# A decode step with cached attention: the first head's K in two pairs of tiles, and the scores' maximum as a running elementwise maximum

## The chip, the core and the metric

The kernel runs on one core of one Trainium2 chip. The metric is the device time of one execution in microseconds (us). A core has several engines that run beside each other: TensorE (PE) multiplies matrices, VectorE (DVE) does elementwise work, reductions and 32x32 transposes, ScalarE (ACT) does casts and functions such as the exponential, and SyncE (SP) issues the large transfers from the chip's memory into the on-chip buffer (SBUF). The transfers themselves are moved by 16 DMA engines. Matrix products land in PSUM, a small accumulation memory.

## What is computed

One token goes through two branches and a gate. Branch A is attention with 32 query heads that share 4 K/V heads of 65536 cached positions each, branch B is a gated MLP. The cut reference:

```python
def _A_ref(x, k_cache, v_cache, wq, wo):          # x 1x1x1024, caches 1x4x65536x128
    q = (x @ wq).reshape(B, Sq, 32, 128).transpose(0, 2, 1, 3)
    k = jnp.repeat(k_cache, 8, axis=1)
    v = jnp.repeat(v_cache, 8, axis=1)
    scores = jnp.einsum('bhqd,bhkd->bhqk', q, k) * 128 ** (-0.5)
    p = softmax(scores, axis=-1)
    o = jnp.einsum('bhqk,bhkd->bhqd', p, v)
    return o.transpose(0, 2, 1, 3).reshape(B, Sq, 4096) @ wo     # wo 4096x1024
...
g = sigmoid((x * gate_w).sum(-1, keepdims=True))
a = _A_ref(x, A_k_cache, A_v_cache, A_wq, A_wo)
b = _B_ref(x, B_w_in, B_w_sp, B_b_sp, B_w_out)    # gelu, layernorm, two products
return g * a + (1 - g) * b
```

All inputs are bf16. K and V together are 134 MB, the weights 28 MB.

## The kernel before

All large inputs pass through one SBUF buffer `kv` with five slots of one tile each. A tile is 128 partitions x 16384 bf16 elements, 4.19 MB; a K head is four tiles (`j` = 0 to 3), and so is a V head. `load(src, shape, at)` starts a transfer into the buffer at slot `at`; `load_kv(src, g, j, at, n)` loads `n` adjacent tiles of head `g`, beginning with tile `j`, in one transfer. Every load is issued by SP in program order, and a load waits until what the slots held before has been used.

```python
P = 128; CT = 128; NKV = 5
kv = big.tile([P, NKV * CT * P], BF16, name="kv")

def load(src, shape, at):
    ...
    ins = nc.sync.dma_start(out=v, in_=src)          # L184

def load_kv(src, g, j, at, n=1):
    h, i = divmod(j, 2)
    rows = src[0, g, 2 * h * CT * P:2 * (h + 1) * CT * P, :].rearrange(
        "(p c) d -> p (c d)", c=2 * CT)
    v = load(rows[:, i * CT * DH:(i + n) * CT * DH], (n * CT * DH,), at)
    return [v[:, i * CT * DH:(i + 1) * CT * DH] for i in range(n)]
```

The first loads are the weights: `B_w_in` at slot 3 (it fills slots 3 and most of 4) and `A_wq` at slots 0 and 1. TensorE uses each as soon as it has landed (`z_ps`, then `q_ps`).

A K tile is worked on in four quarters (`VC` = 4): DVE transposes a quarter in place in blocks of 32x32, reading pairs of bf16 as one int32, and TensorE multiplies it with the query weights `wt`. ACT casts the scores of the tile from PSUM to a bf16 tile `sc` of 128x1024. The row maximum of that tile is taken by DVE with `reduce_max`, put off (`late`) until after the next tile's first transpose.

```python
def k_tile(g, j, kn):
    s_ps = pss.tile([P, 2 * HN], FP32, name="s_ps", tag="s")
    for v in range(VC):
        nc.vector.transpose(out=kb[:, v * n:(v + 1) * n], in_=kb[:, v * n:(v + 1) * n])   # L403
        while late:
            nc.vector.reduce_max(**late.pop())                                            # L405
        for b in range(BP):
            for k in range(2):
                ins = nc.tensor.matmul(s_ps[:, k * HN:(k + 1) * HN], lhsT=wt[...], rhs=kx[...])  # L410
    if g not in mxs:
        mxs[g] = wk.tile([P, NT], FP32, name="mx")
    sct[g, j] = scp.tile([P, CC * B], BF16, name="sc")
    nc.scalar.copy(out=sct[g, j][:], in_=s_ps[:])                                         # L421
    late.append(dict(out=mxs[g][:, j:j + 1], in_=sct[g, j][:], axis=AX.X))
```

When a head's four tiles of scores are there, `stats(g)` brings the maximum of each query row into `nb`, takes the exponential of the four tiles on ACT, and transposes them on DVE for the product with V:

```python
def stats(g):
    nc.vector.reduce_max(**late.pop())                              # L425
    m1 = wk.tile([P, 1], FP32, name="m1")
    nc.vector.reduce_max(out=m1[:], in_=mxs[g][:], axis=AX.X)       # L427
    # PE transpose, max over partitions (L431), copy (L434), PE broadcast, scale (L439) -> nb
    for j in range(NT):
        nc.scalar.activation(out=sct[g, j][:], in_=sct[g, j][:], func=ACT.Exp, ...)   # L443
        nc.vector.transpose(out=ptt[g, j], in_=sct[g, j][:])        # L446
```

`v_tile` (L456, TensorE alone) multiplies these with a V tile, and `head_out` finishes a head. The order of the program:

```python
build_w(0)
for j, n, at in ((0, 1, 2), (1, 1, 3), (2, 1, 0), (3, 1, 1)):
    for i, kn in enumerate(load_kv(A_k_cache, 0, j, at, n)):
        k_tile(0, j + i, kn)
    if j == 1:
        build_w(1)
project(load(B_w_out..., (FC, D), 4), FC, uT, 0, first=True)
stats(0)
for g in range(1, G):
    for h in range(2):
        kn = load_kv(A_k_cache, g, 2 * h, 2 + h, 2)        # slots 2,3 and then 3,4
        for i in ((1, 0), (0, 1))[h]:
            k_tile(g, 2 * h + i, kn[i])
        if h == 0 and g + 1 < G:
            build_w(g + 1)
        vn = load_kv(A_v_cache, g - 1, 2 * h, 0, 2)        # slots 0,1
        v_tile(g - 1, 2 * h, vn[0])
        if h == 1:
            stats(g)
        v_tile(g - 1, 2 * h + 1, vn[1])
    head_out(g - 1)
# ... the last head's V, then A_wo in five pieces
```

Of the kernel before, what the change touches and what calls it, by code (L numbers as in the profile page):

```python
# [8 lines left out]
FP32 = mybir.dt.float32  # L9
BF16 = mybir.dt.bfloat16  # L10
I32 = mybir.dt.int32
ACT = mybir.ActivationFunctionType
ALU = mybir.AluOpType
AX = mybir.AxisListType

P = 128
CT = 128
NKV = 5
B = 32
NB = P // B  # L20
VC = 4
CC = CT // VC
# [7 lines left out]
def kernel(  # L30
# [15 lines left out]
    nc = tc.nc  # L46
# [12 lines left out]
    NT = S // (P * CT)  # L59
# [9 lines left out]
    wk = ctx.enter_context(tc.tile_pool(name="wk", bufs=2))  # L69
    big = ctx.enter_context(tc.tile_pool(name="big", bufs=1))  # L70
# [9 lines left out]
    def same_weights(ins):  # L80
        held.add(ins.ins.name)
# [95 lines left out]
    def load(src, shape, at):  # L177
        n = 1
        for s in shape:
            n *= s  # L180
        v = kv[:, int(at * CT * P):int(at * CT * P) + n]
        if len(shape) == 2:
            v = v.rearrange("p (a b) -> p a b", b=shape[1])
        ins = nc.sync.dma_start(out=v, in_=src)  # L184
        if not first_load:
            first_load.append(ins.ins.name)
        return v
# [7 lines that stand above are left out]
# [60 lines left out]
    for t in range(2):  # L255
        nc.vector.tensor_tensor(  # L256
            out=xm[:, t], in0=xb_ps[:, t * P:(t + 1) * P].rearrange("p (i c) -> p c i", c=KC),
            in1=sel_i[:].unsqueeze(1).to_broadcast([P, KC, P // KC]), op=ALU.mult)
# [51 lines left out]
    for hf in range(2):  # L310
        nc.vector.tensor_tensor(
            out=zm[:, hf], in0=z_ps[:, hf * HN:hf * HN + ZN].rearrange("p (j c) -> p j c", c=FC),
            in1=own_b[:].unsqueeze(2).to_broadcast([P, B, FC]), op=ALU.mult)
    z = wk.tile([P, 2 * FC], FP32, name="z")
    nc.vector.tensor_reduce(out=z[:].rearrange("p (h c) -> p h c", h=2),
                            in_=zm.rearrange("p h j c -> p h c j"), axis=AX.X, op=ALU.add)
# [24 lines left out]
                            op=ALU.subtract)  # L341
# [19 lines left out]
    for k in range(NHB):  # L361
        xs = slice(k * NX // NHB, (k + 1) * NX // NHB)
        nc.vector.tensor_tensor(  # L363
            out=qm[:, xs], in0=q_ps[:, k * HN:(k + 1) * HN].rearrange("p (x j e) -> p x j e",
                                                                   j=B, e=2),
            in1=own_b[:].unsqueeze(1).unsqueeze(3).to_broadcast([P, NX // NHB, B, 2]), op=ALU.mult)
    q1 = wk.tile([P, NX, 2], FP32, name="q1")
    nc.vector.tensor_reduce(out=q1[:], in_=qm.rearrange("p x j e -> p x e j"), axis=AX.X,
                            op=ALU.add)
    q4 = wk.tile([P, NB, NX * 2], BF16, name="q4")  # L370
    nc.vector.tensor_tensor(
        out=q4[:], in0=q1[:].rearrange("p x e -> p (x e)").unsqueeze(1).to_broadcast(
            [P, NB, NX * 2]),
        in1=own_n[:].unsqueeze(2).to_broadcast([P, NB, NX * 2]), op=ALU.mult)
# [6 lines left out]
    for g in range(G):  # L381
        k, t0 = g * T2 // NB, g * T2 % NB
        nc.vector.tensor_copy(out=qs[:, g].rearrange("p b (t h) -> p b t h", t=T2),
                              in_=qv[:, k, t0:t0 + T2].rearrange("p t h b -> p b t h"))

    def build_w(g):
        for v in range(VC):
            nc.vector.tensor_tensor(
                out=wt[g % 2][:, v, :, :, v, :],
                in0=qs[:, g].unsqueeze(2).to_broadcast([P, BP, NB, REP]),  # L390
                in1=own_n[:].unsqueeze(1).unsqueeze(3).to_broadcast([P, BP, NB, REP]),
                op=ALU.mult)

    oa = const.tile([P, OC], BF16, name="oa")
    late = []
    sct, ptt, mxs, lss, o_ps = {}, {}, {}, {}, {}

    def k_tile(g, j, kn):
        kb = kn.bitcast(I32)
        n = CC * DH // 2  # L400
        s_ps = pss.tile([P, 2 * HN], FP32, name="s_ps", tag="s")
        for v in range(VC):
            nc.vector.transpose(out=kb[:, v * n:(v + 1) * n], in_=kb[:, v * n:(v + 1) * n])  # L403
            while late:
                nc.vector.reduce_max(**late.pop())  # L405
            kx = kn[:, v * CC * DH:(v + 1) * CC * DH].rearrange(
                "p (c h k e) -> p h e c k", h=2, k=B, e=2)
            for b in range(BP):
                for k in range(2):
                    ins = nc.tensor.matmul(  # L410
                        s_ps[:, k * HN:(k + 1) * HN],
                        lhsT=wt[g % 2][:, v, b].rearrange("p a v h -> p (a v h)"),
                        rhs=kx[:, b // 2, b % 2, k * CC // 2:(k + 1) * CC // 2, :],
                        start=(v == 0 and b == 0), stop=(v == VC - 1 and b == BP - 1),
                        skip_group_check=True)
                    if k > 0:
                        same_weights(ins)
        if g not in mxs:
            mxs[g] = wk.tile([P, NT], FP32, name="mx")
        sct[g, j] = scp.tile([P, CC * B], BF16, name="sc")  # L420
        nc.scalar.copy(out=sct[g, j][:], in_=s_ps[:])  # L421
        late.append(dict(out=mxs[g][:, j:j + 1], in_=sct[g, j][:], axis=AX.X))

    def stats(g):
        nc.vector.reduce_max(**late.pop())  # L425
        m1 = wk.tile([P, 1], FP32, name="m1")
        nc.vector.reduce_max(out=m1[:], in_=mxs[g][:], axis=AX.X)  # L427
        mt_ps = psm.tile([1, P], FP32, name="mt_ps", tag="m")
        nc.tensor.transpose(mt_ps[:], m1[:], ident_f[:])
        gm = wk.tile([1, REP], FP32, name="gm")  # L430
        nc.vector.tensor_reduce(out=gm[:], in_=mt_ps[:].rearrange("p (a h) -> p h a", h=REP),  # L431
                                axis=AX.X, op=ALU.max)
        gr = wk.tile([1, P // REP, REP], FP32, name="gr")
        nc.vector.tensor_copy(out=gr[:], in_=gm[:].unsqueeze(1).to_broadcast([1, P // REP, REP]))  # L434
        nb_ps = psm.tile([P, 1], FP32, name="nb_ps", tag="m")
        nc.tensor.matmul(nb_ps[:], lhsT=gr[:].rearrange("p a h -> p (a h)"),
                         rhs=ones_f[0:1, 0:1], start=True, stop=True)
        nb = wk.tile([P, 1], FP32, name="nb")
        nc.vector.tensor_scalar(out=nb[:], in0=nb_ps[:], scalar1=-SCALE, scalar2=None,  # L439
                                op0=ALU.mult)  # L440
        lss[g] = wk.tile([P, NT], FP32, name="ls")
        for j in range(NT):
            nc.scalar.activation(out=sct[g, j][:], in_=sct[g, j][:], func=ACT.Exp, scale=SCALE,  # L443
                                 bias=nb[:, 0:1], accum_out=lss[g][:, j:j + 1])
            ptt[g, j] = ptp.tile([P, CC, B], BF16, name="pt")
            nc.vector.transpose(out=ptt[g, j][:].rearrange("p c x -> p (c x)"),  # L446
                                in_=sct[g, j][:])
# [64 lines left out]


    build_w(0)
    for j, n, at in ((0, 1, 2), (1, 1, 3), (2, 1, 0), (3, 1, 1)):
        for i, kn in enumerate(load_kv(A_k_cache, 0, j, at, n)):
            k_tile(0, j + i, kn)
        if j == 1:
            build_w(1)
    project(load(B_w_out.rearrange("(p c) n -> p c n", c=FC), (FC, D), 4), FC, uT, 0, first=True)  # L520
    stats(0)
    for g in range(1, G):
        for h in range(2):
            kn = load_kv(A_k_cache, g, 2 * h, 2 + h, 2)
# [4 lines that stand above are left out]
            vn = load_kv(A_v_cache, g - 1, 2 * h, 0, 2)  # L529
# [5 lines that stand above are left out]
# [61 lines left out]
```

## Time and profile before

| what | value |
|---|---|
| device time, median of 3 (lowest to highest) | 382.2 us (382.17 to 382.49) |
| span of the profiled execution | 380.7 us |
| busy: PE, DVE, ACT | 233.2, 218.5, 39.6 us |
| moved by DMA | 162.17 MB, mean 426 GB/s |
| K and V loads issued by SP: of one tile, of two | 6, 13 |

Busy time is the time in which an engine executed instructions; engines overlap, so the shares do not add up. The rate of the DMA engines is the sum over the 16 of them. In the chain of waits the trace is followed backwards from the last instruction, each time to what released it; a piece "DMA kv" in it runs from the issue of a transfer to its landing, and so contains the time in which the transfer stood in the queue behind earlier ones. In the timeline, a line gives the start and duration of an instruction or of a run of equal ones, and in brackets how long the engine had been idle before it and on what it waited.

### The profile page before, as it was taken

To read this page: it belongs to the slowest core of one execution; us is meant where nothing else is said; L and a number is where in the kernel's file an instruction comes from. 1 tells how busy PE (TensorE), PEld (TensorE's weight loads), DVE (VectorE), ACT (ScalarE), POOL (GpSimd) and SP (SyncE) were. 2 spreads that over 40 slices of the span, in tenths; PEclk is the share of its full clock that TensorE was granted. 3 is DMA by queue.
4 is the path that set the end of the run, shared out by engine and by line. 5 is a ranking of instruction groups with operands and counts; after the bars stand their busy time and mean duration, and the time that the engine had idled before them with its cause. 6 is when DMAs were issued, how large, how long until landed. Compare 5 with 4: busy or idle time off the path is not lost.

```text
span 380.7 us, 2605 instructions
## 1 busy us (share of the span) xinstructions
PE 233.2 (61%) x1395; PEld 56.0 (15%) x800; DVE 218.5 (57%) x211; ACT 39.6 (10%) x55; POOL 4.4 (1%) x10
## 2 busy tenths in 40 slices
PE   0060657876157944796397729871977196839386
PEld 0010101111101210111011101120211011202113
DVE  4133288997597506966977059669970388460040
ACT  1001001110601100114010001050100000500000
POOL 4000000000000000000000000000000000000000
PEclk9995769899759895989688958895989579969789
DMA  9998999999999999999999999999999999999995
GB/s 386 496 420 379 411 438 441 437 483 430 387 420 441 441 436 441 427 441 441 434 436 441 441 427 434 406 423 441 434 434 429 420 441 442 436 410 430 424 443 223
DMA packets 3943, 162.17 MB, mean 426 GB/s; under 512 B 472, under 2 KB 476, under 8 KB 860
## 3 DMA queue, kind: packets, MB, share of 16 engines
q1 hardware_dynamic: 3892, 162.01, 98.8%
q8 instruction: 8, 0.13, 0.1%
q14 instruction: 3, 0.02, 0.0%
q10 hardware_dynamic: 40, 0.01, 0.0%
HBM read 162.01 MB, written 0.00 MB: 426 GB/s over the span
## 4 chain that ended last, share of the span: by engine, by line
DMA 57%; PE 26%; DVE 13%; ACT 2%; issue 1%; SPq 1%; DVEq 0%; ACTq 0%
DMA kv<-in_A_k_cache_dram 43%; PE s_ps L410 21%; DMA kv<-in_A_wo_dram 7%; DVE kv L403 7%; DMA kv<-in_A_v_cache_dram 7%; PE o_ps L456 4%; DVE pt L446 2%; DVE o_sb L470 1%; DVE mx L405 1%; ACT sc L421 1%; ACT sc L443 1%; DVE rowt L466 1%; SPq L184 1%; PE om_ps L476 0%; DVE osum L486 0%
## 5 line engine op out<-in xcount | busy, mean ns | idle before, releaser
L410 PE MATMUL s_ps<-kv,wt 128*128 128x512 bf16 x512 | 141.8, 437 | 80.2 <-DVE kv L403 80.2
L403 DVE STREAM_TRANSPOSE kv<-kv 128x2048 int32<-128x2048 int32 x64 | 142.7, 2281 | 54.3 <-DMA kv<-in_A_k_cache_dram 54.3
L456 PE MATMUL o_ps<-kv,pt 128*64 128x512 bf16 x512 | 61.7, 400 | 7.6 <-DMA kv<-in_A_v_cache_dram 7.6
L410 PEld LDWEIGHTS <-wt 128*128 128x128 bf16 x256 | 27.6, 108 | 195.6 <-issue 138.5
L421 ACT CAST sc<-s_ps 128x1024 bf16<-128x1024 f32 x16 | 16.2, 1012 | 249.9 <-PE s_ps L410 249.9
L456 PEld LDWEIGHTS <-pt 128*64 128x64 bf16 x256 | 16.1, 115 | 50.6 <-issue 48.1
L446 DVE STREAM_TRANSPOSE pt<-sc 128x1024 bf16<-128x1024 bf16 x16 | 18.6, 1217 | 6.8 <-ACT sc L443 6.8
L405 DVE TENSOR_REDUCE mx<-sc 128x1 f32<-128x1024 bf16 x12 | 14.5, 1210 | 9.9 <-ACT sc L421 9.9
L443 ACT ACTIVATE sc<-sc,nb 128x1024 bf16<-128x1024 bf16 x16 | 18.2, 1137 | 12.3 <-DVE nb L439 12.2
L466 DVE TENSOR_TENSOR rowt<-o_ps,own 128x1024 f32<-128x1024 f32 x4 | 4.8, 1195 | 24.9 <-PE o_ps L456 24.9
L476 PE MATMUL om_ps<-o_sb,hsel 128*32 128x128 f32 x8 | 2.3, 386 | 18.3 <-DVE o_sb L470 18.3
L425 DVE TENSOR_REDUCE mx<-sc 128x1 f32<-128x1024 bf16 x4 | 4.9, 1220 | 13.6 <-ACT sc L421 13.6
L296 PE MATMUL q_ps<-kv,xT 128*32 128x512 bf16 x64 | 5.6, 527 | 7.2 <-DMA kv<-in_A_wq_dram 7.2
L252 PE MATMUL xb_ps<-xg,spread 8*128 8x256 bf16 x1 | 0.4, 366 | 13.2 <-DMA xg<-in_gate_w_dram 13.2
L470 DVE TENSOR_REDUCE o_sb<-rowt 128x128 f32<-128x1024 f32 x4 | 7.5, 1872 | 0.1
L363 DVE TENSOR_TENSOR rowt<-q_ps,own_b 128x512 f32<-128x512 f32 x2 | 1.3, 686 | 10.8 <-PE q_ps L296 10.8
L296 PE MATMUL z_ps<-kv,xT 128*32 128x448 bf16 x64 | 5.9, 560 | 0.0
L495 PE MATMUL busy_ps<-wt 128*128 128x512 bf16 x23 | 5.8, 381 | 0.1
L506 PE MATMUL out_ps<-kv,oa 128*32 128x256 bf16 x128 | 4.2, 274 | 2.0 <-DMA kv<-in_A_wo_dram 2.0
L256 DVE TENSOR_TENSOR xm<-xb_ps,sel_i 128x128 f32<-128x128 f32 x2 | 0.5, 287 | 8.0 <-PE xb_ps L252 8.0
L552 ACT CAST out_sb<-out_ps 128x256 bf16<-128x256 f32 x1 | 0.4, 372 | 45.1 <-PE out_ps L506 45.1
L296 PEld LDWEIGHTS <-xT 128*32 128x32 bf16 x64 | 2.6, 136 | 14.6 <-issue 14.6
(90 smaller groups left out, 59.3 us busy)
## 6 DMA issues: line engine op xcount, KB each, us to landing
kv<-in_A_k_cache_dram SPq DMA_DIRECT2D x4, 4096.0 KB, 35.4
kv<-in_A_v_cache_dram SPq DMA_DIRECT2D x2, 4096.0 KB, 26.0
kv<-in_B_w_in_dram SPq DMA_DIRECT2D x1, 7168.0 KB, 19.4
kv<-in_A_wo_dram SPq DMA_DIRECT2D x1, 6144.0 KB
kv<-in_B_w_out_dram SPq DMA_DIRECT2D x1, 3584.0 KB
kv<-in_A_wo_dram SPq DMA_DIRECT2D x1, 1024.0 KB
kv<-in_A_wo_dram SPq DMA_DIRECT2D x1, 512.0 KB
kv<-in_A_wo_dram SPq DMA_DIRECT2D x2, 256.0 KB, 28.2
```

Source lines behind the costliest of these rows:

```text
L296: ins = nc.tensor.matmul(ps[t * B:(t + 1) * B, k * HN:k * HN + n], lhsT=xT[:, i * KH + c:i * KH + c + 1].to_broadcast([P, B]), rhs=w[:, c, ...
L403: nc.vector.transpose(out=kb[:, v * n:(v + 1) * n], in_=kb[:, v * n:(v + 1) * n])
L405: nc.vector.reduce_max(**late.pop())
L410: ins = nc.tensor.matmul(s_ps[:, k * HN:(k + 1) * HN], lhsT=wt[g % 2][:, v, b].rearrange("p a v h -> p (a v h)"), rhs=kx[:, b // 2, b % 2, ...
L421: nc.scalar.copy(out=sct[g, j][:], in_=s_ps[:])
L425: nc.vector.reduce_max(**late.pop())
L443: nc.scalar.activation(out=sct[g, j][:], in_=sct[g, j][:], func=ACT.Exp, scale=SCALE, bias=nb[:, 0:1], accum_out=lss[g][:, j:j + 1])
L446: nc.vector.transpose(out=ptt[g, j][:].rearrange("p c x -> p (c x)"), in_=sct[g, j][:])
L456: ins = nc.tensor.matmul(o_ps[g][hs, e, :], lhsT=ptt[g, j][:, 2 * u:2 * u + 2, :].rearrange("p c x -> p (c x)"), rhs=vx[:, 2 * u + e], sta ...
L466: nc.vector.tensor_tensor(out=om8, in0=o_ps[g][:].rearrange("p e (v d) -> p (e v) d", d=DH), in1=own_8[:].unsqueeze(2).to_broadcast([P, 2 ...
L470: nc.vector.tensor_reduce(out=o_sb[:], in_=om8.rearrange("p x d -> p d x"), axis=AX.X, op=ALU.add)
L495: ins = nc.tensor.matmul(ps[:, :HN], lhsT=w[:, :P], rhs=w[:, :HN], start=True, stop=True, skip_group_check=True)
```

## The change

There are two parts. The first head's K, loaded in four transfers of one tile each, is loaded in two transfers of two tiles each, at the same slots. The maximum of a head's scores, before a reduction along the columns of each of four score tiles and a small one over the four results, becomes a running elementwise maximum of the score tiles in bf16 (the first tile stands for itself), and one reduction along the columns at the end. The pair loads make rows of 64 KB out of rows of 32 KB and the number of transfers smaller; the running maximum is meant to take work off VectorE.

```diff
+    mx = big.tile([P, CC * B], BF16, name="mx")
+
+    def running_max(g, sc):
+        if g in mxs:
+            nc.vector.tensor_tensor(out=mx[:], in0=mxs[g][:], in1=sc[:], op=ALU.max)
+            mxs[g] = mx
+        else:
+            mxs[g] = sc
...
             while late:
-                nc.vector.reduce_max(**late.pop())
+                running_max(*late.pop())
...
-        if g not in mxs:
-            mxs[g] = wk.tile([P, NT], FP32, name="mx")
         sct[g, j] = scp.tile([P, CC * B], BF16, name="sc")
         nc.scalar.copy(out=sct[g, j][:], in_=s_ps[:])
-        late.append(dict(out=mxs[g][:, j:j + 1], in_=sct[g, j][:], axis=AX.X))
+        late.append((g, sct[g, j]))

     def stats(g):
-        nc.vector.reduce_max(**late.pop())
+        running_max(*late.pop())
         m1 = wk.tile([P, 1], FP32, name="m1")
         nc.vector.reduce_max(out=m1[:], in_=mxs[g][:], axis=AX.X)
...
-    for j, n, at in ((0, 1, 2), (1, 1, 3), (2, 1, 0), (3, 1, 1)):
-        for i, kn in enumerate(load_kv(A_k_cache, 0, j, at, n)):
+    for j, at in ((0, 2), (2, 0)):
+        for i, kn in enumerate(load_kv(A_k_cache, 0, j, at, 2)):
             k_tile(0, j + i, kn)
-        if j == 1:
+        if j == 0:
             build_w(1)
```

## The prediction

> **What bounds the kernel now.** I read the page's slices first, then the chain of waits in order of time, then SyncE's timeline. The page:
>
> ```profile
> DMA  9998999999999999999999999999999999999995
> q1 hardware_dynamic: 3892, 162.01, 98.8%
> kv<-in_B_w_in_dram SPq DMA_DIRECT2D x1, 7168.0 KB, 19.4
> ```
>
> All slices but the last are full: the 16 DMA engines are busy nearly always, while PE and DVE are busy for some 60%. So the question is only whether the queue is ever empty. The chain of waits gives landings as issue plus duration:
>
> ```profile
> 1.16 48.79 DMA kv<-in_A_k_cache_dram
> ...
> 73.12 33.87 DMA kv<-in_A_k_cache_dram
> ...
> 119.04 26.66 DMA kv<-in_A_k_cache_dram
> ...
> 197.42 25.72 DMA kv<-in_A_k_cache_dram
> ...
> 273.80 26.94 DMA kv<-in_A_k_cache_dram
> ```
>
> The reader is to see landings at 106.99, 145.70, 223.14 and 300.74. Between the first two lie two transfers of 8.39 MB: 16.78 MB in 38.7 us, 433 GB/s. Between 145.70 and 300.74 lie eight: 67.1 MB in 155.0 us, 433 GB/s again. No time is lost there; a pair takes 19.37 us, a tile 9.68. Of the 162.01 MB, at 433 GB/s, come 374 us; some 7 us of the span are start, landing and tail. The first transfer (7.34 MB, 16.95 us of moving) landed 19.4 us after its issue at 0: about 2.45 us for issue and landing around the data. A transfer issued later than 2.45 us before its predecessor lands leaves the DMA engines idle. That gives each load a latest moment, and SyncE's timeline the moment it really had:
>
> ```profile
> 73.12 0.33 SPq L184 DMA_DIRECT2D kv<-in_A_k_cache_dram  x1
> 94.83 0.33 SPq L184 DMA_DIRECT2D kv<-in_A_v_cache_dram  x1
> 119.04 0.33 SPq L184 DMA_DIRECT2D kv<-in_A_k_cache_dram  x1
> 137.69 0.33 SPq L184 DMA_DIRECT2D kv<-in_A_v_cache_dram  x1
> ```
>
> These are head 1's first K pair, head 0's first V pair, head 1's second K pair, head 0's second V pair. Predecessors land at 106.99-19.37 = 87.6, 106.99, 126.35 and 145.70; latest moments 85.2, 104.5, 123.9 and 143.3. The slack is 12.1, 9.7, 4.9 and 5.6 us. So the kernel is bound by the stream, with five us in hand at the third of these.
>
> **What the Trainium skill says.** "VectorE: DVE Perf Modes", section on the perf-mode tier table, has `tensor_reduce` at one element per cycle only, and `tensor_tensor` on bf16 in SBUF at two. The trace agrees on the first: 1.21 us for 1024 columns (the L405 row below). The second isn't in this trace; half of the reduction's columns and its fixed part, by the cycle counts of that page's side-by-side section some (512+158)/0.96 = 0.70 us, is an estimate, and I use 0.65 since the operations here overlap a little. "DMA: Bandwidth & Descriptors", section on the anatomy of one DMA, states a fixed part of about 2 us per transfer, measured for another issuing path; my 2.45 us from this trace's first load is near it and is used. The same page's section on where 436 GB/s comes from puts the ceiling at 435; the 433 measured here is at it, so nothing is left to gain in rate.
>
> **The change part by part.** The views of VectorE (groups, then the timeline from 49 to 118 us):
>
> ```profile
> L405 DVE TENSOR_REDUCE mx<-sc 128x1 f32<-128x1024 bf16 x12 | 14.5, 1210 | 9.9 <-ACT sc L421 9.9
> ```
> ```profile
> 49.97 8.89 DVE L403 STREAM_TRANSPOSE kv<-kv 128x2048 int32<-128x2048 int32 x4 [1.03 <-DMA kv<-in_A_k_cache_dram]
> ...
> 59.77 2.31 DVE L403 STREAM_TRANSPOSE kv<-kv 128x2048 int32<-128x2048 int32 x1 [0.90 <-DMA kv<-in_A_k_cache_dram]
> ...
> 95.88 1.22 DVE L425 TENSOR_REDUCE mx<-sc 128x1 f32<-128x1024 bf16 x1 [3.03 <-ACT sc L421]
> 97.13 0.16 DVE L427 TENSOR_REDUCE m<-mx 128x1 f32<-128x4 f32 x1
> ...
> 101.52 4.64 DVE L446 STREAM_TRANSPOSE pt<-sc 128x1024 bf16<-128x1024 bf16 x4 [2.65 <-ACT sc L443]
> 107.02 11.09 DVE L403 STREAM_TRANSPOSE kv<-kv 128x2048 int32<-128x2048 int32 x5 [0.85 <-DMA kv<-in_A_k_cache_dram]
> ```
>
> *The maximum.* Removed per head: four reductions of 1.21 and a small one of 0.16, 5.0 us. Added: three elementwise maxima of 0.65 and one reduction of 1.22, 3.2 us. VectorE saves 1.8 us a head, 7 us in all, from an engine that is 57% busy. On the critical order inside `stats` it costs: 0.65+1.22 in place of 1.22+0.16, half a us more. In the later heads the transfers have 4 to 5 us of slack, so neither sign reaches the end: 0.
>
> *The pairs.* The bytes are the same, and two transfers fewer save next to nothing: from the first tile's landing at 49.95 to 106.99 come 24.64 MB in 57.04 us, 432 GB/s, with 32 KB rows; at 433 it would be 0.1 us less. What moves is when compute may begin. A pair lands as a whole, so VectorE starts at 59.8, where the second tile landed before, and not at 49.97. From there I add up, a quarter's transpose being 2.22 us (8.89/4):
> - Pair one: eight transposes, 17.8, to 77.6; the weights for head 1 (0.86) to 78.4. The second pair lands at 106.99 less 27.83 us for what follows it (3.67 and 8.39 MB), 79.2.
> - Pair two: eight transposes (17.8), two elementwise maxima (1.3), and a wait for ACT as before (0.7) give 99.0; before it was 92.85. PE follows by 2 us, so head 0's V pair is issued at 101.0, 3.5 us ahead of its latest moment 104.5.
> - `stats(0)`: cast to 102.1, maximum 0.65, reduction 1.22, so 103.95 against 97.3. The rest, as before: 4.2 us to the first transpose of the exponentials and 4.64 for the four, to 112.85.
> - So head 1's K starts on VectorE at 112.85, and not at 107.02: 5.8 us later. Before, from that start to the issue of the second K pair went 12.0 us (107.02 to 119.04). Now it is issued at 124.85.
>
> Its latest moment is 123.9. It comes 0.95 us late, and the DMA engines idle for that long. Later loads get their slack back: VectorE waits 17 us for this pair in the trace of before, and drops work after it. So the delay goes to the end once and doesn't grow. The sum: +0.95 for the late load, -0.1 for fewer and longer rows, 0 for the maxima; I take off another 0.2, since 2.45 us includes the program's start and may be less in the stream. 382.2 + 0.65, say 382.8.
>
> **The rivals.** *Nothing happens.* If my slip is a us too large (PE following faster, the pair landing earlier than 59.8) the load is still in time, and the time is 382.0 to 382.3. The narrow margin speaks for it: 0.95 us out of a sum of eight terms. *The stream gets a bit faster.* Between the landing of `A_wq` (38.8, when `q_ps` begins) and of the first K tile (49.95) go 11.15 us where 9.68 would do. If these 1.5 us belong to the short rows or to the number of transfers, the pairs bring them back: 381 or so. Against it: the three single tiles behind it run at full rate, so it looks like one engine that was disturbed once. *The elementwise maximum runs at one element per cycle.* Then each is 1.2 us, the chain to the issue is 1.7 us longer and the loss 2.5 us: 384.5. Against it stands the skill's table. *VectorE as the bound* (7 us less work showing in the time) has nothing for it: its longest idle stretches are waits on K transfers.
>
> **Range and chances.** The mechanism bounds the loss between 0 and about 2.5 us, and the recovery of the lost 1.5 us is the only way down. I take 381.4 to 384.2. Two per cent is 7.6 us; no rival comes near it. Faster 0.01, same 0.975, slower 0.015.
>
> **What would show it right or wrong.** In the changed trace, VectorE's first K transpose starts near 59.8; the elementwise maxima take about 0.65 us each; head 1's first K transpose starts near 112.9 and waits for VectorE's own work, not for DMA; the second K pair of head 1 is issued near 124.9 and lands near 146.5 and not at 145.7; all later landings are shifted by that same amount. Wrong it would be if that landing is no later than before (the queue never ran dry), or if the landing of head 1's first K pair, 106.99, moves.

## The result, and the profile after

The changed kernel takes 383.6 us (median of 6 runs, 383.04 to 384.36) against 382.2 us before: a ratio of 1.0036, with a 95% interval of 1.0023 to 1.0049. It is 1.4 us slower.

The page of the changed kernel, the lines that answer to those shown of before: the DMA slices, the load queue, below it the instruction queue q8 (8 packets of 16 KB, as in the kernel before), which is taken up at the end, and the new groups of VectorE.

```profile
DMA  9999999899998999999999999999999999999995
q1 hardware_dynamic: 3604, 162.01, 98.2%
q8 instruction: 8, 0.13, 0.1%
```
```profile
L402 DVE TENSOR_TENSOR mx<-mx,sc 128x1024 bf16<-128x1024 bf16 x8 | 5.5, 692 | 16.2 <-ACT sc L428 16.2
...
L434 DVE TENSOR_REDUCE m<-mx 128x1 f32<-128x1024 bf16 x4 | 4.9, 1220 | 0.1
...
L402 DVE TENSOR_TENSOR mx<-sc 128x1024 bf16<-128x1024 bf16 x4 | 2.6, 649 | 0.0
```

The elementwise maximum takes 0.65 to 0.69 us, little more than half of a reduction (1.21), and VectorE's busy time falls from 218.5 to 211.3 us. But the load queue is busy for 98.2% of a longer span (98.8% before), and two slices have an 8 that was a 9, the later of them from 115 to 124 us. SyncE's timeline of the changed kernel says what is late there (start, duration):

```profile
79.37 0.33 SPq L184 DMA_DIRECT2D kv<-in_A_k_cache_dram  x1
100.95 0.33 SPq L184 DMA_DIRECT2D kv<-in_A_v_cache_dram  x1
125.05 0.33 SPq L184 DMA_DIRECT2D kv<-in_A_k_cache_dram  x1
139.38 0.33 SPq L184 DMA_DIRECT2D kv<-in_A_v_cache_dram  x1
```

The first three of these loads are issued 6 us later than before. The chain of waits, where each piece again runs from issue to landing:

```profile
125.05 23.27 DMA kv<-in_A_k_cache_dram
...
159.99 27.03 DMA kv<-in_A_k_cache_dram
...
198.07 27.65 DMA kv<-in_A_k_cache_dram
...
237.94 26.49 DMA kv<-in_A_k_cache_dram
...
276.02 27.11 DMA kv<-in_A_k_cache_dram
...
314.73 27.11 DMA kv<-in_A_v_cache_dram
```

Head 1's second K pair lands at 148.32, where it landed at 145.70 before: 2.62 us later. Head 1's first K pair lands at 106.90 (106.99 before), so the loss lies between these two. The DMA line for 120 to 130 us alone, before and after, shows it (a digit stands for 0.25 us, and a packet counts where it starts):

```profile
DMA  6060609900606609990060660999060606099006
```
```profile
DMA  6066096606006600000000079970600000099990
```

In the changed kernel no packet starts from 123.5 to 125.75 us; only the V pair's last packets, of 2.42 us each, are still under way there.

After 148.32 the landings are 187.02, 225.72, 264.43, 303.13 and 341.84, one per 38.7 us, which is two pairs at 433 GB/s. No more is lost, and nearly nothing is given back: the last load of `A_wo` lands at 380.82 against 378.54, 2.28 us later. The profiled execution is the longest of the six (384.36); the others lost less, as is taken up below.

VectorE's timeline of the changed kernel shows why that load is late:

```profile
59.73 17.66 DVE L412 STREAM_TRANSPOSE kv<-kv 128x2048 int32<-128x2048 int32 x8 [10.95 <-DMA kv<-in_A_k_cache_dram]
...
79.15 2.31 DVE L412 STREAM_TRANSPOSE kv<-kv 128x2048 int32<-128x2048 int32 x1 [0.99 <-DMA kv<-in_A_k_cache_dram]
...
112.75 17.62 DVE L412 STREAM_TRANSPOSE kv<-kv 128x2048 int32<-128x2048 int32 x8
```

The last line has no bracket: head 1's first K had long landed, and VectorE came to it only when it was done with head 0, 5.7 us later than before. Its first tile sets free the slot that the second pair waits for.

### The profile page after: what moved, and what is told of

It reads as the page before. It is cut to its first block, busy times and chain, and to the rows that moved or that the text cites. A ratio compares the mean times of both kernels' runs of the same rounds, so it can differ in the third digit from the quotient of the medians.

```text
span 382.9 us, 2605 instructions
## 1 busy us (share of the span) xinstructions
PE 223.3 (58%) x1397; PEld 54.5 (14%) x800; DVE 211.3 (55%) x207; ACT 39.6 (10%) x55; POOL 4.4 (1%) x10
## 3 DMA queue, kind: packets, MB, share of 16 engines
q1 hardware_dynamic: 3604, 162.01, 98.2%
## 4 chain that ended last, share of the span: by engine, by line
DMA 68%; PE 18%; DVE 10%; issue 3%; ACT 1%; SPq 0%; DVEq 0%; ACTq 0%
DMA kv<-in_A_k_cache_dram 43%; PE s_ps L419 14%; DMA kv<-in_A_wq_dram 10%; DMA kv<-in_A_wo_dram 7%; DVE kv L412 7%; DMA kv<-in_A_v_cache_dram 7%; PE o_ps L463 2%; PE q_ps L296 1%; DVE pt L453 1%; DVE mx L402 1%; ACT sc L428 1%; SPq L184 0%; ACT L450 0%; ACT sc L450 0%; DVE m L434 0%
## 5 line engine op out<-in xcount | busy, mean ns | idle before, releaser
L419 PE MATMUL s_ps<-kv,wt 128*128 128x512 bf16 x512 | 131.8, 411 | 90.8 <-DVE kv L412 90.5
L419 PEld LDWEIGHTS <-wt 128*128 128x128 bf16 x256 | 26.2, 102 | 197.6 <-issue 119.6
L453 DVE STREAM_TRANSPOSE pt<-sc 128x1024 bf16<-128x1024 bf16 x16 | 18.6, 1217 | 6.8 <-ACT sc L450 6.8
L402 DVE TENSOR_TENSOR mx<-mx,sc 128x1024 bf16<-128x1024 bf16 x8 | 5.5, 692 | 16.2 <-ACT sc L428 16.2
L434 DVE TENSOR_REDUCE m<-mx 128x1 f32<-128x1024 bf16 x4 | 4.9, 1220 | 0.1
```

The lines of the kernel that those rows point to most:

```text
L402: nc.vector.tensor_tensor(out=mx[:], in0=mxs[g][:], in1=sc[:], op=ALU.max)
```

## The experiments

The theory (A): the pairs make VectorE finish head 0 later, so head 1's second K pair is issued after its latest moment and the DMA engines run dry. Rival B: the elementwise maxima cost the time. Rival C: pair loads are slower in themselves.

**The maxima alone.** The edit on the changed kernel:

```diff
-    for j, at in ((0, 2), (2, 0)):
-        for i, kn in enumerate(load_kv(A_k_cache, 0, j, at, 2)):
+    for j, n, at in ((0, 1, 2), (1, 1, 3), (2, 1, 0), (3, 1, 1)):
+        for i, kn in enumerate(load_kv(A_k_cache, 0, j, at, n)):
             k_tile(0, j + i, kn)
-        if j == 0:
+        if j == 1:
             build_w(1)
```

> The running maximum with the first head's K in four single tiles as before. Theory A (late load: the pairs start head 0 later, head 1's second K pair is issued too late and the DMA queue runs dry): the first K transpose is back near 50, head 1's second K pair is issued near 119 and lands near 145.7, time 382.0 to 382.3. Rival B (the elementwise maxima and the longer chain before the exponentials cost the time): 383.3 to 383.9, the same as with both parts.

382.04 us against 382.28, ratio 0.9993 (0.9985 to 1.0001). The profiled execution of this run was a slow one (769.67 us) and is not read; a second measurement of the kernel has a trace:

> The running maximum with single tiles once more, for its trace. Late load: head 1's second K pair is issued near 119, against a latest moment of 145.7-23.1 = 122.6, lands near 145.7, and the time is 381.9 to 382.2. If the maxima cost anything by themselves: over 382.5.

381.89 us against 382.25, ratio 0.9990 (0.9982 to 0.9999). The load in question is issued at 117.89 and lands at 146.19. Rival B falls: the maxima cost nothing, and by this run save about a tenth of a per cent (0.01 to 0.18).

**The pairs alone.** The kernel before with the two pair loads of the change and its own four reductions.

> The first head's K in two pairs, with the four column reductions as before. Theory A: the reductions hold VectorE up more than the maxima did (waits for the casts of the first tile, 1.22 in place of 0.65), so head 1's second K pair is issued near 127.7, some 2.7 us later than with both parts; time near 386.3 (385 to 387). Rival B: as before the change, 382.2, since the maxima are gone. Rival C (pair transfers are slower in themselves): as with both parts, 383.6.

387.96 us, ratio 1.0150 (1.0134 to 1.0166): 5.7 us slower, 1.7 us more than expected and outside the expected range. The load is issued at 128.02 and lands at 151.03, 5.33 us later than before. VectorE's timeline of this kernel:

```profile
59.93 11.08 DVE L403 STREAM_TRANSPOSE kv<-kv 128x2048 int32<-128x2048 int32 x5 [11.31 <-DMA kv<-in_A_k_cache_dram]
72.19 1.22 DVE L405 TENSOR_REDUCE mx<-sc 128x1 f32<-128x1024 bf16 x1 [1.17 <-ACT sc L421]
```

The reduction of the first tile stands in the midst of the pair and waits for its cast, which the running maximum doesn't do: the first tile there has no instruction of its own. VectorE comes to the second pair at 80.71 and not at 79.15, and the later reductions and their waits add as much again until head 1 (115.72 and 112.75). So the two parts of the change belong together: the pairs cost 5.7 us, and the maxima, which bring next to nothing on their own, take 4.3 of them back (387.96 to 383.61). At the issue of the late load it is 2.97 us; the rest of the 4.3 is not traced.

**Both parts, with VectorE's order changed.** The four transposes of head 0's exponentials are moved behind head 1's first K tile; `p_tile` is the transpose of L453 as a function of its own.

```diff
     for j in range(NT):
         nc.scalar.activation(out=sct[g, j][:], in_=sct[g, j][:], func=ACT.Exp, ...)
-        ptt[g, j] = ptp.tile([P, CC, B], BF16, name="pt")
-        nc.vector.transpose(...)
+        if g > 0:
+            p_tile(g, j)
...
                 k_tile(g, 2 * h + i, kn[i])
+                if g == 1 and (h, i) == (0, 1):
+                    for j in range(NT):
+                        p_tile(0, j)
```

> Both parts of the change, but the four transposes of head 0's exponentials stand on VectorE behind head 1's first K tile and not ahead of it (4.6 us of VectorE work moved, none removed). Theory A: head 1's first K transpose starts when its K lands, near 107; its second K pair is issued near 119, and the loss is gone: 381.8 to 382.2. Rival B and rival C: nothing of what they hold to be the cause is changed, 383.6.

381.87 us against 382.28, ratio 0.9990 (0.9984 to 0.9997). VectorE's timeline of this kernel:

```profile
106.54 8.89 DVE L412 STREAM_TRANSPOSE kv<-kv 128x2048 int32<-128x2048 int32 x4 [1.62 <-DMA kv<-in_A_k_cache_dram]
115.36 4.58 DVE L457 STREAM_TRANSPOSE pt<-sc 128x1024 bf16<-128x1024 bf16 x4
```

VectorE waits for head 1's K again (the bracket is back), the second pair is issued at 118.61 and lands at 145.19, and the whole loss is gone, with pairs and maxima both in the kernel. Rival C falls with it.

**Lateness without either part.** The kernel before, with 4, 6 or 9 transposes of a score tile into a scratch tile ahead of head 1's first K:

```diff
     stats(0)
+    extra = const.tile([P, CC * B], BF16, name="extra")
+    for i in range(6):
+        nc.vector.transpose(out=extra[:], in_=sct[0, 0][:])
```

> The kernel before with four extra transposes ahead of head 1's first K. With six, that K pair's successor was issued at 124.61; a transpose there costs 1.26 us, so with four it is issued near 122.1. If the fixed part between issue and landing is 3.7 us in the stream (as the two starved kernels showed), the latest moment is 145.7-19.37-3.7 = 122.6: just in time, 382.2 to 382.5. If the loss grew with VectorE's work and not with lateness, two thirds of what six cost: 383.7.

> The kernel before, with six extra transposes of a score tile (1.16 us each, 7.0 us in all, into a scratch tile that nothing reads) on VectorE ahead of head 1's first K. VectorE had 0.85 us idle there, so head 1's second K pair is issued 6.1 us later, near 125.1, as in the changed kernel. Theory A: 383.5 to 384.5 without either part of the change, and the landing of that pair near 148. Rivals B and C: 382.2, since neither maxima nor pairs are in it.

> Nine extra transposes: the load is issued near 128.4 and lands near 151.5. Late load, slope one: 3.8 us more than with six, 388.1 (387.5 to 389). If later slack gives part of it back: under 387.

384.05 us, 384.35 us and 388.74 us (ratios 1.0048, 1.0068 and 1.0172, each within 0.002). The chain of waits with six and with nine:

```profile
124.61 23.08 DMA kv<-in_A_k_cache_dram
```
```profile
129.68 23.06 DMA kv<-in_A_k_cache_dram
```

Six and nine came as the theory had it (with nine the load was issued 1.3 us later than expected, and the time still lies in the range); four missed, 384.05 where 382.2 to 382.5 was expected. By its time alone it lies nearer to the rival named there, a loss that grows with VectorE's work (383.7); but the kernel with moved transposes has all the VectorE work of the changed kernel and no loss, and the trace puts the load with four on the same line of issue and landing as the others. That trace has the load at 123.61 and not at 122.1: VectorE reached head 1's K with four extra transposes only 0.7 us before it did with six (111.53 and 112.25), since in head 0 the second tile's later transposes began at 64.18 in one trace and at 63.09 in the other, each behind a reduction that waited for the first tile's cast, and the last reduction waited 3.79 and 3.03 us for its own. Head 0's compute thus differs by a us between kernels with the same code there. In the kernel before, 3.6 us of slack hide that; in a kernel that is late already it goes to the end, which fits the wider spread of its runs (383.04 to 384.36, against 382.15 to 382.49).

**Which pair.** The running maximum, with only one half of head 0's K as a pair: `((0, 2, 2), (2, 1, 0), (3, 1, 1))` or `((0, 1, 2), (1, 1, 3), (2, 2, 0))` as tile, number and slot.

> The running maximum, with tiles 0 and 1 of head 0 as a pair and tiles 2 and 3 as two single loads. Late load: VectorE has tile 2 in hand when it is done with the first pair, at 78.2 and not at 79.2, so head 1's second K pair is issued 1.0 us earlier than with two pairs, near 124.1: 382.5 to 383.0. If it is the late begin of compute (59.7) that counts: 383.6.

> The running maximum, with tiles 0 and 1 as single loads and tiles 2 and 3 as a pair. VectorE starts near 50 again, but runs out of tiles near 70 and waits for the pair until 79.1; from there everything is as with two pairs. Late load: 383.6, head 1's second K pair issued near 125. If it is the late begin of compute that counts: 382.2.

383.04 us (ratio 1.0028, 1.0019 to 1.0038) and 384.43 us (1.0058, 1.0046 to 1.0071). With the second half as a pair VectorE starts at 49.77 again, and it brings nothing. VectorE's timeline of that kernel:

```profile
59.55 8.89 DVE L412 STREAM_TRANSPOSE kv<-kv 128x2048 int32<-128x2048 int32 x4 [0.90 <-DMA kv<-in_A_k_cache_dram]
...
78.84 2.31 DVE L412 STREAM_TRANSPOSE kv<-kv 128x2048 int32<-128x2048 int32 x1 [9.62 <-DMA kv<-in_A_k_cache_dram]
...
112.93 17.62 DVE L412 STREAM_TRANSPOSE kv<-kv 128x2048 int32<-128x2048 int32 x8
```

The ten idle us have moved from ahead of the first tile to ahead of the third, and head 1 starts at 112.93, as with two pairs. What counts is how much work is left for VectorE when the last tile lands, and either pair adds to it: the load is issued at 117.89 with neither, at 122.89 with the first half as a pair, at 124.91 with the second, at 125.05 with both. The first-half kernel was 1.2 us earlier than expected: from VectorE's start on head 1 (112.06) to the issue it took 10.8 us, where it took 12.3 with two pairs.

**Single tiles with the order changed.** The maxima, single tiles, and the moved transposes.

> The running maximum, single tiles for head 0's K, and the transposes of head 0's exponentials behind head 1's first K tile. If only lateness counts, nothing is late in it, and it is where the pairs with moved transposes were: 381.8 to 382.1. If the pair loads themselves gave the 0.4 us that that kernel lay below the one before: 382.2 to 382.4.

381.94 us against 382.25, ratio 0.9993 (0.9984 to 1.0001). So the 0.4 us that pairs with moved transposes lie below the kernel before aren't owed to the pairs. The three kernels with the running maximum in which nothing is late lie at 381.9 to 382.0; what gives them this tenth of a per cent isn't shown, since their profiled spans (380.5 to 380.8) are those of before (380.7).

All of it in one table: when head 1's second K pair was issued, when it landed by the chain of waits, and the time.

| kernel | issue | landing | between | time |
|---|---|---|---|---|
| maxima alone (second run) | 117.89 | 146.19 | 28.30 | 381.89 |
| singles, transposes moved | 118.44 | 145.46 | 27.02 | 381.94 |
| pairs, transposes moved | 118.61 | 145.19 | 26.58 | 381.87 |
| before | 119.04 | 145.70 | 26.66 | 382.2 |
| first half as a pair | 122.89 | 145.99 | 23.10 | 383.04 |
| 4 extra transposes | 123.61 | 147.04 | 23.43 | 384.05 |
| 6 extra transposes | 124.61 | 147.69 | 23.08 | 384.35 |
| second half as a pair | 124.91 | 147.90 | 22.99 | 384.43 |
| the change | 125.05 | 148.32 | 23.27 | 383.61 |
| pairs alone | 128.02 | 151.03 | 23.01 | 387.96 |
| 9 extra transposes | 129.68 | 152.74 | 23.06 | 388.74 |

Up to an issue at 119.04 the landing doesn't depend on the issue. From 122.89 on it is the issue plus 23.0 to 23.4, whatever made it late, with pairs or without, with maxima or reductions. The first row of these, the first half as a pair, is at the edge: its landing lies among those of the kernels that are in time, and its 0.85 us show only later (head 2's second K pair lands at 224.09, and at 223.14 before).

## Why the prediction was right, and which term was too small

- *The bound.* Right. The rate was 433 GB/s before and after, and the only loss is at one load.
- *The maxima.* Right: two elements per cycle by the Trainium skill's page on VectorE ("VectorE: DVE Perf Modes", perf-mode tier table), from which 0.70 us was estimated and 0.65 used; 0.649 and 0.692 measured. Standing alone they moved the time by about 0.1%. That they would take 4.3 us out of the cost of the pairs was not seen, since the pairs weren't worked out without them.
- *The pairs, VectorE's sum.* Right to 0.2 us at each step: head 0's V pair issued at 100.95 (101.0 predicted), head 1's K begun at 112.75 (112.85), its second pair issued at 125.05 (124.85). The words "what moves is when compute may begin" tell only half: the run with the second half as a pair begins at 49.77 and is as late. The sum itself waited for the second pair's landing, and was right.
- *The latest moment.* This is the term that was mis-sized. The prediction took 2.45 us for issue and landing around the data, from the first load of the program. In the starved kernels issue to landing is 22.99 to 23.43 us, and 19.37 of it data: 3.6 to 4.1 us, mostly 3.7. So the latest moment was 145.70-23.1 = 122.6 and not 123.9, the slack before was 3.6 us and not 4.9, and the profiled load came 2.5 us late and not 0.95. The 0.2 us taken off "since 2.45 may be less in the stream" went the wrong way. With 3.7 in its place the sum gives +2.2, and 384.4, which is the profiled execution (384.36); the median of the runs is 0.8 us below it.
- *What the 3.7 us are.* The traces hold sixteen completion times for a load, one from each DMA engine, and the load has landed with the last. With six extra transposes, fifteen of the late pair's engines are done from 145.85 to 146.50 and the last at 147.69; with nine, from 150.95 to 151.69 and at 152.74. Counted to the fifteenth engine the part beside the data is 2.5 and 2.6 us, about that of the first load, whose sixteen are done from 18.94 to 19.41. In between, one packet of 16 KB of the queue q8 starts (at 143.42 and 148.40), just where one engine ends a packet of its own, and that engine's next packet takes 2.9 to 3.0 us in place of 2.42. All seven starved kernels have such a packet within this load's time, the first load has none. In five of the seven that engine is the last by 0.7 to 1.3 us; with four extra transposes and with the first half as a pair another engine, which began late, ends within 0.2 us of it. So 2.45 was not far off for most of the engines; what the prediction left out is that one of the sixteen comes later. This is read from the traces; no run takes the packet away.
- *The rival of the lost 1.5 us.* Wrong, and instructive. After the change, too, the first K load lands 20.8 us behind `A_wq` (38.94 to 59.70) where 19.37 would do. Neither rows nor number of transfers bring it back. The objection in the prediction, one engine that was disturbed once, is what the traces show: in the kernel before, fifteen engines are done with the first K tile by 48.50 and the last at 49.95, and a packet of q8 starts at 43.08 (at 43.31 in the changed kernel). So the delay of one engine that the latest moment left out stood in the prediction, under another heading.

The measured time lies in the range of 381.4 to 384.2, with a loss of 1.4 us where 0.65 was forecast. Of the signs named beforehand one missed for the same reason: the landing, 146.5 foretold and 148.32 measured. That the median still lies in the range is owed to its width.

## What to carry to other kernels

In a kernel whose transfers fill the span, work out for each load its slack, the latest moment (landing of the one before, less the fixed part) against the real issue, and take the fixed part from loads in mid-program too, not from the first alone: a load has landed only with its slowest DMA engine, which here could be more than 1 us behind the other fifteen. A change that makes loads larger or fewer spends slack in compute that waits for the whole of them; it can be earned back by letting the engine that frees the next slot do that work first. Judge two parts of a change by running each alone: here one costs 5.7 us, and the other is worth 4.3 us beside it and nearly nothing without.

## What was not expected of the hardware

A K pair that was issued into a queue that had run dry took 3.7 us beside its data, also with nine extra transposes, where it was issued at 129.68, some 3 us after its predecessor should have landed (126.4, by the full rate from 106.99). So it isn't owed to transfers still under way. The first load of the program took 2.45 us. By the traces most of the difference lies in one of the sixteen DMA engines: a packet of 16 KB of the instruction queue, which has 0.1% of the DMA engines' time on the page, sets one engine back by about 1.4 us (0.9 to 1.0 until that engine's next packet of the load starts, and half a us in that packet), and the landing of a load of 8.39 MB waits for it. With a full queue it needn't show: in the kernel before, such a packet starts at 136.15, within the time of the same K pair, and its landing (145.70) is still two pairs at the full rate behind 106.99. Whether a kernel without these packets would be spared the delay was not tried.
